# Splitting the opening batch of a DFT-and-GEGLU kernel by residue parity, with reordered loads and a later second batch

## The chip, the cores and the metric

The kernel runs on one core of one Trainium2 chip. The metric is the device time of one execution in microseconds; lower is better. All times in this text are microseconds unless another unit is named. Engines are called PE (matrix multiply), DVE (vector), ACT (activation), POOL (general purpose) and SP (which here only issues transfers).

## What is computed

The input x has 8 batches of 3008 rows with 256 channels. Each batch goes through a Fourier transform along the rows and one along the channels; the real part is then the input of a gated feed-forward block with 256 inputs, 1536 hidden units and 256 outputs.

```python
batch, seq, dim = (8, 3008, 256)
X = np.fft.fft(x, axis=1)
X = np.fft.fft(X, axis=2)
x = X.real.astype(np.float32).reshape(24064, 256)
g = x @ w_gate
gelu = 0.5 * g * (1.0 + erf(g * inv_sqrt2))
val = x @ w_val
out = (gelu * val @ w_out).astype(np.float32)
```

## The kernel before

**Row transform.** 3008 is 64 x 47. A batch is loaded in thirds (`load_x`, line 199) into three `xin` tiles. `fold_x` (211) adds and subtracts mirrored channels, which gives an even and an odd part of 128 channels each, and copies the two single channels (0 and 128). The first stage is `a_step(b, k)` (462): twelve steps for a batch, each with two matmuls against the table `G` and one copy into `S1`. The result has 128 rows for each of 24 slots. It goes through a scratch tensor `z` in HBM to change its layout: `z_write` (481) writes some of the 24 slots, `z_read` (489) reads thirds of it into `Ap`, every fourth partition from 0, 1 or 2. In `Ap` a group g of 0 to 31 is the row number modulo 32. The second stage is `b_steps(b, eo, q)` (499): a matmul of 47 columns against `TP`, `TQ`, `T0P` or `T0Q` for each group, eight groups into one PSUM bank (q is 0 to 3), for the even (`eo` 0) and odd part. The copies out of PSUM (`evac`, or `evac_top` and `evac_rest`) write `Y`, whose column is 32 m + g. All four q of a parity are needed for any 512 neighbouring columns of `Y`. For batch 0 the odd part is followed by one-column matmuls for the single channel; for later batches that row comes from `n_turn`, `n_step` and `n_read`.

**Channel transform.** It is folded into the weights: `gen_w` (397) multiplies the cast weights `wb` (`cast_w`, 391) by the table `CW` and gives `WE` and `WOP`, and `WOM`, which is `WOP` times minus two, so that it can be added onto a finished sum to turn the plus rows into the mirrored minus rows.

**Feed-forward.** Work is cut into units (b, chunk, fc): batch, chunk of `Y` columns, block of 128 hidden units; twelve units a chunk, three chunks a batch. `CH` (73) has the order of the chunks: the 481 columns from 1024, then 0 to 511, then 512 to 1023. A unit has five matmuls (`val_even`, `gate_minus`, `gate_plus`, `val_odd`), and six in the first chunk of batch 0, where the row `NQs` that DVE uses in the other units (`ev`, line 606) is not there yet. The products go to `h`; `plus` on DVE, `minus` on POOL. A chunk's second layer, `l2_steps` (689), starts after its twelfth unit, at six to eight matmuls against `Wo_sb` a unit.

**Order.** Every engine call goes through `_InOrder`, so each engine works in program order; a late operand stops everything behind it on that engine. SP's queue is in order too, and a transfer may wait in it for another transfer's landing. The loop over units (849) has the plan written out by hand: `extra` and `a_first` (828, 834) say at which unit of batch 0 a `gen_w` or an `a_step` of batch 1 is done; `first` and `evens` (840 to 846) say where the steps of `b_steps` are put (`fills`); `loads` (856) where the x of the batch after next is loaded.

**Opening.** Before the loop (766 to 827) the core loads x and a third of the weights, makes its tables, does the whole first and second stage of batch 0, and `gen_w` of the first 512 hidden units. `warm` issues matmuls whose result nobody uses; eight of them take the tile `gate`, read back from `z`, as weights. `cols_t` (247) works out column vectors from the partition number by rounding on DVE; `phase_t` and `sin_t` make the tables of the second stage from them. The transfers in this part are, in SP's order:

```python
z_read(0, 0); z_read(0, 1)        # gate read here
z_read(0, 2)
load_w(512, 1); load_w(512, 0); load_x(1, 0)
load_w(1024, 1); load_w(1024, 0); load_x(1, 1); load_x(1, 2)
```

`load_wo` (287) is issued on POOL after `cast_w(512)`, ahead of the folds of batch 1, which POOL does at units 0 to 11.

Of the kernel before, what the change touches and what calls it, by code (L numbers as in the profile page):

```python
# [9 lines left out]
FP32 = mybir.dt.float32  # L10
# [27 lines left out]
def kernel(  # L38
# [34 lines left out]
    CH = [(1024, NCOL - 1024), (0, 512), (512, 512)]  # L73
    MID = 24
# [26 lines left out]
    lone = const_pool.tile([128, NFC], BF16)  # L101

# [12 lines left out]
    col_q = const_pool.tile([128, 3], FP32)  # L115
    row_w = const_pool.tile([128, 3], FP32)
    row_b = const_pool.tile([128, 3], FP32)
    col_t = const_pool.tile([128, 1], FP32)
    col_k = const_pool.tile([128, 1], FP32)
    col_w = const_pool.tile([128, 1], FP32)  # L120
    col_m = const_pool.tile([128, 1], FP32)
    col_top = const_pool.tile([128, 1], FP32)
    col_bot = const_pool.tile([128, 1], FP32)
# [71 lines left out]
    def z_tile():  # L195
        return dram.tile([HJ, 128, C], BF16, tag="z", bufs=2, name="z")
# [14 lines left out]
    def fold_x(b, i, eng, a0=0, an=8, other=None):  # L211
# [8 lines left out]
        (other or eng).tensor_copy(  # L220
            _sub(xf, [[C, an], [128, 2]], o0), _sub(xt, [[C, an], [128, 2]], a0 * C))
# [17 lines left out]
    iota(col_q, [[0, 3]], 0, 1)  # L239
    for i in range(3):  # L240
        d = 4 << i
        pool.memset(row_w[:, i : i + 1], 1.0 / d)
        pool.memset(row_b[:, i : i + 1], (1.0 - d) / (2 * d))
    pool.tensor_tensor(col_q, col_q, row_w, op=ALU.mult)
    pool.tensor_tensor(col_q, col_q, row_b, op=ALU.add)

    def cols_t():
        f4, f8, f16 = (col_q[:, i : i + 1] for i in range(3))
        vec.tensor_scalar(col_q, col_q, MAGIC, None, op0=ALU.add)
        vec.tensor_scalar(col_q, col_q, MAGIC, None, op0=ALU.subtract)  # L250
        vec.scalar_tensor_tensor(col_t, f4, -4.0, col_p, op0=ALU.mult, op1=ALU.add)
        vec.scalar_tensor_tensor(col_bot, f8, -2.0, f4, op0=ALU.mult, op1=ALU.add)
        vec.scalar_tensor_tensor(f8, f16, -2.0, f8, op0=ALU.mult, op1=ALU.add)
        vec.scalar_tensor_tensor(col_j, col_t, 8.0, f16, op0=ALU.mult, op1=ALU.add)
        vec.scalar_tensor_tensor(col_j, f8, 24.0, col_j, op0=ALU.mult, op1=ALU.add)
        vec.tensor_scalar(col_j, col_j, 1.0 / N2, None, op0=ALU.mult)
        for o, b0 in ((0, 0.25), (2 * N2, 0.0)):
            vec.tensor_scalar(
                _sub(quat, [[1, 2 * N2]], o), _sub(col_bot, [[0, 2 * N2]], 0),
                0.25, b0, op0=ALU.mult, op1=ALU.add)  # L260
        vec.tensor_scalar(col_k, col_t, 3.0, None, op0=ALU.is_lt)
        vec.tensor_scalar(col_w, col_k, -TWO_PI, None, op0=ALU.mult)
        vec.tensor_tensor(col_bot, col_bot, col_k, op=ALU.mult)
        vec.tensor_tensor(col_top, col_k, col_bot, op=ALU.subtract)

    TO = 4 * N2
    iota(_sub(rowt, [[2 * N2, 2], [1, 2 * N2]], 0), [[0, 2], [1, 2 * N2]], 0, 0)
    iota(_sub(rowt, [[NJ, 2], [1, MID]], TO), [[0, 2], [1, MID]], 0, 0)
    iota(_sub(rowt, [[NJ, 2], [1, MID - 1]], TO + MID), [[0, 2], [1, MID - 1]], 1, 0)
    pool.memset(_sub(rowt, [[NJ, 2]], TO + NJ - 1), 0.0)  # L270
    pool.memset(_sub(quat, [[1, NJ]], TO), 0.25)
    pool.memset(_sub(quat, [[1, NJ]], TO + NJ), 0.0)
    TG = TO + 2 * NJ
    iota(_sub(rowt, [[NG, 2], [1, NG]], TG), [[0, 2], [-11, NG]], 0, 0)
    pool.memset(_sub(quat, [[1, NG]], TG), 0.25)
    pool.memset(_sub(quat, [[1, NG]], TG + NG), 0.5)
    wst = []

# [703 lines left out]
```

## Time and profile before

| what | value |
|---|---|
| median of 3 runs | 631.41 (631.33 to 631.5) |
| profiled execution | 629.75 |
| its span | 627.6 |
| first matmul of unit 0 | 28.60 |
| PE busy in the span | 606.0 |
| PE busy from 0 to 28.60 | 16.08 |
| PE busy from 28.60 to 54.20 | 24.02 of 25.60 |
| data moved from HBM and to it | 45.08 MB and 37.25 MB |

In the lines below, a row of the timeline has the start, the duration, the engine, the operation with what it writes and reads (out<-in), the shape, and after x how many of them were merged. In brackets stands the time that the engine was idle before, and what ended it. SPq and POOLq rows are issues of transfers, not the transfers themselves. Matmuls overlap, so the distance from one start to the next is the price of a matmul, not its duration. The profiled execution is one execution; the median belongs to others, and differs from it by 1.66.

### The profile page before, as it was taken

Reading aid. Unit: us, or ns where it says so; the run is one execution under the profiler, and the core shown is the slowest. Engines: PE = TensorE matmul, PEld = TensorE weight load, DVE = VectorE, ACT = ScalarE, POOL = GpSimd, SP = SyncE. Lnnn points to the kernel's source line nnn. Section 1 sums busy time; section 2 is a strip of 40 time slices with the busy share of each in tenths; the row PEclk is TensorE's granted clock in tenths of the full one; section 3 lists DMA queues with packets and bytes.
Section 4 is the critical chain, followed back from the end, with each engine's and each line's share of the span. In section 5 each row is a group of like instructions: output and inputs, shape, how many; then the busy total and the mean of one; then the engine's idle time right before and its main releaser. Section 6 shows DMA issues by size and latency. Waiting matters only on the chain.

```text
span 627.6 us, 12916 instructions
## 1 busy us (share of the span) xinstructions
PE 606.0 (97%) x4522; PEld 402.0 (64%) x4580; DVE 541.5 (86%) x654; ACT 471.8 (75%) x956; POOL 449.7 (72%) x480
## 2 busy tenths in 40 slices
PE   3899999999999999999999999999999999999997
PEld 2445666766666666766667666666667666666665
DVE  7688988898888998888988898889898898999991
ACT  8687778877788777877778777887778777766662
POOL 8296987769868789687787788687885555556552
PEclk9999999999999999999999999999999999999999
DMA  8997523653237512574246533366223612222113
GB/s 311 348 283 234 153 64 113 173 185 98 76 101 218 194 49 74 177 223 121 51 119 173 190 103 74 104 208 204 56 60 93 194 45 50 60 50 52 39 47 85
DMA packets 65458, 82.39 MB, mean 131 GB/s; under 512 B 8298, under 2 KB 58986, under 8 KB 62578
## 3 DMA queue, kind: packets, MB, share of 16 engines
q1 hardware_dynamic: 63682, 80.65, 42.4%
q0 software_dynamic: 1552, 0.79, 0.9%
q8 instruction: 36, 0.59, 0.4%
q14 instruction: 28, 0.23, 0.1%
q10 hardware_dynamic: 160, 0.13, 0.1%
HBM read 45.08 MB, written 37.25 MB: 131 GB/s over the span
## 4 chain that ended last, share of the span: by engine, by line
PE 91%; DMA 3%; DVE 3%; ACT 1%; issue 1%; POOL 0%; SPq 0%; ACTq 0%; DVEq 0%; POOLq 0%
PE ps_o L25 38%; PE ps_g L25 28%; PE ps_v L25 19%; PE ps_d L25 6%; DMA xin<-in_x_dram 3%; DVE h L25 1%; DVE S L25 0%; DMA z<-S 0%; ACT glp L25 0%; DVE xf L25 0%; ACT glm L25 0%; ACT S L25 0%; POOL xf L25 0%; SPq L25 0%; DVE WOM L25 0%
## 5 line engine op out<-in xcount | busy, mean ns | idle before, releaser
L25 POOL TENSOR_TENSOR h<-glm,dv 128x1024 bf16<-128x1024 bf16 (+1 forms) x138 | 290.9, 2108 | 153.2 <-DVE dv L25 110.0
L25 PE MATMUL ps_o<-Wo_sb,h 128*128 128x256 bf16 x2136 | 277.7, 272 | 0.5 <-DVE S L25 0.3
L25 DVE SCALAR_TENSOR_TENSOR ev<-nq,WN,ps_v 128x512 f32<-128x512 bf16 (+1 forms) x276 | 202.6, 734 | 62.3 <-PE ps_v L25 43.5
L25 ACT ACTIVATE glm<-ps_g 128x512 bf16<-128x512 f32 (+1 forms) x288 | 169.4, 588 | 110.0 <-PE ps_g L25 70.8
L25 PEld LDWEIGHTS <-h 128*128 128x128 bf16 x2208 | 210.8, 97 | 54.6 <-issue 0.9
L25 ACT ACTIVATE glp<-ps_g 128x512 bf16<-128x512 f32 (+1 forms) x288 | 169.9, 590 | 9.9 <-PE ps_g L25 0.3
L25 DVE TENSOR_TENSOR h<-glp,ps_v 128x1024 bf16<-128x1024 bf16 (+2 forms) x150 | 172.9, 1153 | 4.9 <-ACT glp L25 2.7
L25 DVE SCALAR_TENSOR_TENSOR dv<-ev,ps_v 128x1024 f32<-128x1024 f32 (+1 forms) x138 | 164.8, 1194 | 0.0
L25 POOL TENSOR_TENSOR xf<-xin 128x254 bf16<-128x254 f32 x168 | 118.3, 726 | 1.8 <-DMA xin<-in_x_dram 1.8
L25 PE MATMUL ps_g<-Y,WOM 128*128 128x512 bf16 (+1 forms) x288 | 107.7, 374 | 0.3
L25 PE MATMUL ps_v<-Y,WOP 128*128 128x512 bf16 (+1 forms) x288 | 107.7, 374 | 0.0
L25 PE MATMUL ps_v<-Y,WE 128*128 128x512 bf16 (+1 forms) x282 | 105.7, 375 | 0.1
L25 PE MATMUL ps_g<-Y,WOP 128*128 128x512 bf16 (+1 forms) x278 | 103.9, 374 | 1.7
L25 PE MATMUL ps_g<-Y,WE 128*128 128x512 bf16 (+1 forms) x249 | 92.9, 373 | 0.0
L25 PEld LDWEIGHTS <-WOP 128*128 128x128 bf16 x576 | 55.7, 97 | 52.8 <-ACT WOP L25 0.4
L25 PEld LDWEIGHTS <-WE 128*128 128x128 bf16 x576 | 56.0, 97 | 30.9 <-issue 0.6
L25 ACT ACTIVATE osb<-ps_o 128x512 f32<-128x512 f32 x93 | 54.8, 589 | 17.6 <-PE ps_o L25 13.6
L25 PEld LDWEIGHTS <-Ap 128*128 128x128 bf16 (+1 forms) x561 | 40.9, 95 | 33.8 <-issue 0.2
L25 ACT ACTIVATE S<-ps_d 128x512 bf16<-128x512 f32 x80 | 47.4, 593 | 0.1
L25 PEld LDWEIGHTS <-G 128*128 128x128 bf16 x213 | 20.8, 100 | 33.2 <-issue 11.8
L25 ACT ACTIVATE Y<-ps_d 128x192 bf16<-128x192 f32 (+4 forms) x142 | 34.0, 340 | 0.5 <-PE ps_d L25 0.5
L25 PEld LDWEIGHTS <-WOM 128*128 128x128 bf16 x300 | 29.2, 97 | 4.9
(140 smaller groups left out, 262.7 us busy)
## 6 DMA issues: line engine op xcount, KB each, us to landing
out_dram<-osb SPq DMA_DIRECT2D x358, 64.0 KB
xin<-in_x_dram SPq DMA_DIRECT2D x16, 1024.0 KB
Ap<-z SPq DMA_DIRECT2D x24, 512.0 KB
xin<-in_x_dram SPq DMA_DIRECT2D x8, 896.0 KB
z<-S SPq DMA_DIRECT2D x7, 768.0 KB
z<-S SPq DMA_DIRECT2D x8, 512.0 KB
nq<-nrow SPq DMA_DIRECT2D x8, 376.2 KB
z<-S SPq DMA_DIRECT2D x11, 256.0 KB
```

What stands on the lines that cost most here:

```text
L25: return lambda *a, **k: self._tc.keep_in_program_order(call(*a, **k))
```

## The change

The change concerns batch 0, the opening, and where batch 1's stages are put; a few of its parts hold for all batches.

- The scratch `z` is split in two by the parity of the row (`z_tile(half)`); a half is written from every second partition of `S1`. `Ap` holds the sixteen even groups first, then the odd ones. For all batches each `z_write` and `z_read` becomes one transfer for each half. In the opening only half 0 is written and read at first; half 1 is written in one transfer later, and read back in three.
- Batch 0 has its own chunk order and its own column order (`CH0`, `evac_first`, `halved_windows`, `store_apart`): columns 0 to 511 of `Y` are the even groups, 512 to 1023 the odd ones, and the rest is as it was. So the first chunk needs q 0 and 1 only. `b_steps` for q 2 and 3 is done at units 7 to 10. The stores of these chunks go to every second row of the output.
- Group 0, whose two column ranges now go to different places, is done by a matmul in each of two banks (q 0 and q 1).
- The column vectors of `cols_t` come from five matmuls of one row (`prow`, made on POOL by `rows_t`); most of the DVE operations of `cols_t` and the tile `gate` are gone.
- On POOL `cols_c` and `phase_c` move ahead of the folds, the tables and the clearing of `Ap` behind the first of them; `cast_w(1024)` comes directly after `cast_w(512)`, and `load_wo` moves to unit 4.
- In the opening `WOM` is made from `WOP` in SBUF after all four `gen_w`, and one copy moves from ACT to DVE. There are fewer `warm` matmuls: 7 after the first stage instead of 5, 2 and 10 within it, and 3 and 4 instead of 4 and 8 before the second stage.
- The weights of the hidden units 512 to 1535 are loaded ahead of x of batch 1; half 1 of `z` is written after the first third of that x.
- Batch 1's `a_step`s are at units 9 to 18 instead of 4 to 13, its `z_read`s at units 15, 17 and 20, its first `b_steps` at unit 22 instead of 21, and `n_first(0)` at unit 8 instead of 0. `load_x(2, ...)` is at units 8, 15 and 20 instead of 8, 12 and 18.
- The last rows of batch 0's first two chunks are gathered in a tile `aside` on POOL.

```diff
     CH = [(1024, NCOL - 1024), (0, 512), (512, 512)]
+    CH0 = [(0, 512), (1024, NCOL - 1024), (512, 512)]
...
-    def z_tile():
-        return dram.tile([HJ, 128, C], BF16, tag="z", bufs=2, name="z")
+    def z_tile(half):
+        return dram.tile([HJ, 64, C], BF16, tag=f"z{half}", bufs=2, name=f"z{half}")
...
+    def rows_t():
+        row = lambda i, pat, off=0: _sub(prow, pat, 128 * i + off, 0, 1)
+        iota(row(0, [[16, 8], [8, 2], [4, 2], [1, 4]]), [[1, 8], [24, 2], [0, 2], [8, 4]], 0, 0)
+        slots = [[8, 16], [4, 2], [1, 4]]
+        for i, (base, sign) in enumerate(((0, 1), (0, 1), (1, -1))):
+            iota(row(1 + i, slots), [[0, 16], [sign, 2], [0, 4]], base, 0)
+        pool.memset(row(4, [[1, 129]]), 1.0)
+        pool.memset(row(2, [[128, 3], [4, 32]], 3), 0.0)
 
     def cols_t():
...
+        ps = ps_o()
+        for i in range(5):
+            pe.matmul(ps[:, i : i + 1], _sub(prow, [[1, 128]], 128 * i, 0, 1),
+                      _sub(prow, [[1, 1]], 640, 0, 1), start=True, stop=True)
+        vec.tensor_copy(cols, ps[:, :5])
+        vec.tensor_scalar(col_j, cols[:, 0:1], 1.0 / N2, None, op0=ALU.mult)
+        vec.tensor_scalar(col_w, cols[:, 4:5], -TWO_PI, None, op0=ALU.mult)
+
...
+        copy = act.copy if eng is None else eng.tensor_copy
+        on_half(ps, copy((WE, WOP)[eo][:, i, fs], ps))
+        if eo:
+            if f0:
+                on_half(ps, vec.tensor_scalar(
+                    WOM[:, i, fs], ps, col_m, None, op0=ALU.mult))
+            else:
+                odd_evacs.append(lambda: vec.tensor_scalar(
+                    WOM[:, i, fs], WOP[:, i, fs], col_m, None, op0=ALU.mult))
 
...
+            st[b]["z"] = [z_tile(half) for half in range(2)]
+        S1 = st[b]["S1"]
+        for half in halves:
+            z = st[b]["z"][half]
+            dst = ap_replace(
+                z[0:1, 0, :], ap=[[C, 64], [64 * C, nj], [1, C]], offset=z[j0, 0:1, :].offset)
+            rows = _sub(S1, [[C, nj], [1, C]], j0 * C, half, 64)
+            p_step, p_count = rows.ap[0]
+            src = ap_replace(
+                rows, ap=[[2 * p_step, p_count]] + [list(a) for a in rows.ap[1:]],
+                offset=rows.offset)
+            sync.dma_start(out=dst, in_=src)
+
+    def z_read(b, third, halves=(0, 1)):
+        n = NG // 2 * C
+        for half in halves:
+            z = st[b]["z"][half]
+            src = ap_replace(
+                z[0:1, 0, :], ap=[[n, 32], [1, n]], offset=z[8 * third, 0:1, :].offset)
+            p_step = Ap[:, :, :].ap[0][0]
+            dst = ap_replace(
+                Ap[:, :, :], ap=[[4 * p_step, 32], [1, n]],
+                offset=Ap[:, :, :].offset + third * p_step + half * n)
+            sync.dma_start(out=dst, in_=src)
...
+                pos = (8 * q + gi) % 16 + NG // 2 * (q // 2) if gi < 8 else 0
+                g = 2 * (pos % 16) + pos // 16
+                w = _sub(Ap, [[1, 1 if m1 else 128]], pos * C + eo * 128)
...
+                    lo, hi = (MID, N2) if gi else (0, MID)
                     keep((pe.matmul(
-                        ps[r, 0:N2], w, t[:, 0:N2], start=True, stop=True)))
-                    keep(pe.matmul(ps[r, 8 * N2 : 8 * N2 + 1], w, t[:, N2 : N2 + 1],
-                                         start=True, stop=True))
+                        ps[r, o + lo : o + hi], w, t[:, lo:hi], start=True, stop=True)))
+                    if gi == 0:
+                        keep(pe.matmul(ps[r, 8 * N2 : 8 * N2 + 1], w, t[:, N2 : N2 + 1],
+                                             start=True, stop=True))
...
+        gh, first, n = q // 2, q % 2 * 8, 9 if q == 1 else 8
+
+        def part(lo, hi, halved):
             ps = box["ps"]
             if Ys[b] is None:
                 Ys[b] = Y_tile()
-            copy(
-                _sub(Ys[b], [[32, MID], [1, 8]], eo * YW + 8 * q),
-                _sub(ps, [[1, MID], [N2, 8]], 0))
+            f = 1 if q == 0 and lo >= MID else 0
+            p = first - (1 if q == 1 and lo >= MID else 0)
+            nn = (n if lo >= MID else 8) - f
+            at = 512 * gh + 16 * lo + p if halved else \
+                32 * lo + 2 * p + (1 - gh if lo >= MID else gh)
+            m, s = (16, 1) if halved else (32, 2)
+            copy(_sub(Ys[b], [[m, hi - lo], [s, nn]], eo * YW + at),
+                 _sub(ps, [[1, hi - lo], [N2, nn]], lo + f * N2))
+
+        def evac_first():
+            if gh:
+                part(0, 32, True)
+            else:
+                part(0, MID, True)
+                part(MID, 32, True)
 
         def evac_rest():
...
+            part(32, N2, False)
             if q == 0:
-                copy(
-                    _sub(Y, [[32, n2]], eo * YW + 32 * MID + 31), ps[:, MID:N2])
-                copy(
-                    _sub(Y, [[1, 1]], eo * YW + NCOL - 1), ps[:, 8 * N2 : 8 * N2 + 1])
-
-        steps = [mm(gi, False) for gi in range(8)]
+                copy(_sub(Ys[b], [[1, 1]], eo * YW + NCOL - 1),
+                     box["ps"][:, 8 * N2 : 8 * N2 + 1])
+
+        order = [*range(1, n), 0] if q == 0 else range(n)
+        steps = [mm(gi, False) for gi in order]
...
+    def halved_windows(ci):
+        h = hs[(0, ci)]
+        gh = CH0[ci][0] // 512
+        row = lambda m: 64 * m + (1 if gh else 2 * (m >= MID))
+        out = [(h, 128 * w, (row(8 * w), 8), None) for w in range(4)]
+        out += [(h, 128 * w, (T - row(8 * (8 - w) - 1) - 30, 8), None) for w in range(4, 8)]
+        if gh == 0:
+            pool.tensor_copy(aside[:, :, :], h[:, :, 896:1024])
+            return out[:7]
+        return out
...
     for i in (1, 0):
         load_w(0, i)
+    cols_c()
+    for t in range(NCH):
+        phase_c(t)
+    def clear(i):
+        pool.memset(Ap[:, 16 * i : 16 * i + 16, :].bitcast(FP32), 0.0)
+
...
     phase_g(0)
     phase_g(1)
-    cols_c()
     sin_g(0)
     sin_g(1)
     turn_g()
-    pool.tensor_copy(col_k, _sub(reds[1], [[1, 1]], 0))
     for i in range(3):
-        fold_x(0, i, vec, other=pool)
-        if i < 2:
-            pool.memset(Ap[:, 16 * i : 16 * i + 16, :].bitcast(FP32), 0.0)
-        else:
-            for t in range(NCH):
-                phase_c(t)
+        fold_x(0, i, vec, single=False)
+        if i == 0:
+            singles(0)
+            singles(1)
+            rows_t()
+            clear(0)
+            singles(2)
+            tables()
+            clear(1)
+        elif i == 2:
+            cols_t()
         for k in range(4 * i, 4 * i + 4):
             a_step(0, k)
-            if i == 0 and k == 3:
-                z_write(0, 0, 8)
-            elif i and k % 2:
-                z_write(0, 2 * k - 2, 4)
-        warm((5, 2, 10)[i])
-    z_read(0, 0)
-    z_read(0, 1)
-    gate = work.tile([128, 128], BF16, tag="gate", bufs=1, name="gate")
-    sync.dma_start(out=gate[:, :], in_=ap_replace(
-        st[0]["z"][0:1, 0, :], ap=[[C, 128], [1, 128]], offset=st[0]["z"][0:1, 0, :].offset))
-    z_read(0, 2)
+            if k % 2:
+                z_write(0, 2 * k - 2, 4, (0,))
+    warm(7)
+    z_read(0, 0, (0,))
+    z_read(0, 1, (0,))
+    z_read(0, 2, (0,))
     for i in (1, 0):
         load_w(512, i)
-    load_x(1, 0)
     for i in (1, 0):
         load_w(1024, i)
+    load_x(1, 0)
+    z_write(0, 0, HJ, (1,))
+    for i in range(3):
+        z_read(0, i, (1,))
     load_x(1, 1)
     load_x(1, 2)
     reduce_c()
-    cols_t()
-    pt = phase_t()
+    quats()
     sin_c()
     cast_w(0)
+    pt = phase_t()
     gen_w(0, 1, 0, ps_g)
     gen_w(0, 1, 1, ps_vh)
+    gen_w(0, 0, 0, ps_g, vec)
     sin_t(*pt)
-    gen_w(0, 0, 0, ps_g)
     gen_w(0, 0, 1, ps_vh)
     act.activation(col_f[:, :], col_p[:, :], AF.Gelu)
-    warm(4)
-    warm(8, gate[:, :])
+    for w in odd_evacs:
+        w()
+    odd_evacs.clear()
+    warm(3)
+    warm(4, TP)
     later_evacs = []
     for eo in range(2):
-        for q in range(4):
-            steps, evac, evac_top, evac_rest = b_steps(0, eo, q)
+        for q in range(2):
+            steps, evac, evac_first, evac_rest = b_steps(0, eo, q)
             for s in steps:
                 s()
-            if eo:
-                evac_rest()
-                later_evacs.append(evac_top)
-            else:
-                evac()
+            evac_first()
+            later_evacs.append(evac_rest)
     cast_w(512)
-    load_wo()
-    extra = {1: [lambda: cast_w(1024)], 13: [gen_tf]}
-    for n, turn in ((0, (ps_o, ps_d, ps_o, ps_d)), (1, (ps_o, ps_o, ps_d, ps_o))):
+    cast_w(1024)
+    extra = {4: [load_wo], 13: [gen_tf]}
+    for n, turn in ((0, (ps_o, ps_d, ps_o, ps_d)), (1, (ps_o, ps_d, ps_o, ps_d))):
         for j, bank in enumerate(turn):
-            extra.setdefault(4 * n + j, []).append(
+            extra.setdefault(4 + j if n else (1, 2, 2, 3)[j], []).append(
                 lambda f0=512 + 512 * n, i=1 - j // 2, eo=j % 2, bank=bank: gen_w(f0, i, eo, bank))
-    extra[7].append(gen_wn)
-    a_first = {4: (0,), 5: (1,), 12: (10,), 13: (11,), 14: (12,), 15: (13,)} | {
-        8 + j: (2 + 2 * j, 3 + 2 * j) for j in range(4)}
+    extra.setdefault(10, []).append(gen_wn)
+    a_first = {9: (0,), 10: (1, 2), 11: (3, 4)} | {12 + j: (5 + j,) for j in range(7)}
+    reads_first = {15: 0, 17: 1, 20: 2}
 
     NU = len(units)
     PER = NU // B
...
-    first = {23: ["n"], 21: [(1, 0, 0, 4)], 22: [(1, 0, 4, 8)]} | {
+    first = {22: [(1, 0, 0, 4)], 23: [(1, 0, 4, 8)]} | {
         23 + q: [(1, q, 0, 8)] for q in range(1, 4)}
+    first[24].append("n")
     plan = [first | evens, later | evens]
+    second_half = {7: (1, 2), 8: (1, 3), 9: (0, 2), 10: (0, 3)}
...
-            loads = (0, 14, 19) if b else (8, 12, 18)
+            loads = (0, 14, 19) if b else (8, 15, 20)
...
-                    if k in (8, 10, 13):
+                    if b and k in (8, 10, 13):
                         z_read(b + 1, (8, 10, 13).index(k))
+                if b == 0 and i in reads_first:
+                    z_read(1, reads_first[i])
```

## The prediction

> **What bounds the kernel now.** I read the page first, then the busy time by stretches, then the timeline of the opening and of the SP queue, and the trace's gaps on PE. One profiled execution took 629.75 us, its span 627.6; the median of the runs is 631.41, so 1.66 is added to whatever the sum gives for that execution.
>
> ```profile
> span 627.6 us, 12916 instructions
> PE 606.0 (97%) x4522; PEld 402.0 (64%) x4580; DVE 541.5 (86%) x654; ACT 471.8 (75%) x956; POOL 449.7 (72%) x480
> ```
> ```profile
> 0.00:28.60 28.60, 16.08 (x159) 9.26 (x161) 22.13 (x65) 20.53 (x47) 16.66 (x45) 1.00 0.91 324
> 28.60:54.20 25.60, 24.02 (x146) 11.99 (x147) 21.40 (x38) 21.24 (x42) 23.80 (x48) 1.00 0.84 256
> 75.00:150.00 75.00, 74.57 (x574) 50.54 (x581) 65.37 (x73) 58.25 (x121) 60.08 (x65) 1.00 0.44 130
> ```
> Columns: stretch, its length, busy PE, PEld, DVE, ACT, POOL (instructions), granted clock, DMA share, GB/s. From 75 on PE is busy 74.57 of 75: the end moves only by what PE does or waits for. 12.5 of the idle time lies before 28.60, where the DMA share is 0.91; another 1.58 until 54.20.
>
> ```profile
> 8.88 0.58 PE L25 MATMUL ps_g<-xf,G 128*128 128x256 bf16 x2 [8.88 <-DVE xf L25]
> ...
> 12.46 0.38 PE L25 MATMUL ps_g<-xf,G 128*128 128x256 bf16 x2
> ...
> 14.95 2.02 POOL L25 CAST wb<-wst 128x1024 bf16<-128x1024 f32 x2
> ...
> 15.96 0.68 DVE L25 CAST S<-ps_o 128x512 bf16<-128x512 f32 x1
> ...
> 23.60 1.90 PE L25 MATMUL ps_d<-G,gate 128*128 128x512 bf16 x8 [2.30 <-DMA gate<-z]
> ...
> 25.17 3.38 PEld L25 LDWEIGHTS <-Ap 128*128 128x128 bf16 x99 [0.16 <-issue]
> ...
> 28.60 0.38 PE L25 MATMUL ps_v<-Y,WE 128*128 128x481 bf16 x1
> ...
> 29.17 0.36 PE L25 MATMUL ps_g<-Y,WOP 128*128 128x481 bf16 x1
> ```
> The first stage's last result is copied by 16.64, but its use as Ap starts at 25.17: write to z and read back. Then 99 steps take 3.43, and unit 0 starts.
>
> ```profile
> 17.21 1.17 SPq L25 DMA_DIRECT2D Ap<-z  x2
> 18.43 0.57 SPq L25 DMA_DIRECT2D gate<-z  x1
> 19.88 0.45 SPq L25 DMA_DIRECT2D Ap<-z  x1
> ...
> 29.52 0.31 SPq L25 DMA_DIRECT2D nrow<-Y  x1
> 37.59 0.36 SPq L25 DMA_DIRECT2D nq<-nrow  x1
> ...
> 56.56 0.37 SPq L25 DMA_DIRECT2D z<-S  x1
> ...
> 63.50 0.48 SPq L25 DMA_DIRECT2D Ap<-z  x1
> ```
> The SP queue shows how long a small transfer takes behind large ones: nq could be issued only 8.07 after nrow, and batch 1's last Ap read 6.94 after its z write.
>
> **Opening.** The six folds on DVE end at 13.67 as before (row 6.38 7.29). The third group of a_steps then needs four pairs at 0.22 (pitch at 12.46, 12.68, 12.90) or 0.43 (pitch at 8.88 to 10.11), since warm-ups go, and copies of 0.6: last S1 at 15.3 to 16.1; I take 16.0. The last write of half 0 has 4 x 64 x 512 B; the last whole write took 3.11 from issue to landing behind others, so 1.5 to 3.1, taken 2.4. The last half read replaces one that took at most 5.3 (19.88 to 25.17) behind two double ones and gate: 2.3 to 5.3, taken 3.1. Ap's first half is there at about 21.6 (limits 19.1 to 24.5). There are 54 steps instead of 99 (18 even, 36 odd), at 3.43/99 = 0.035: 1.9, until 23.5.
>
> The other way into unit 0 is POOL and ACT. POOL now does phase_c (2.43) and col_c before the folds, but rows_t (four iotas, two memsets, 1.0 from rows of 0.1 to 0.3), two clears of 1.82, singles and tables after x lands, so cast_w(0) (2.02) ends at about 18.3 against 16.97. Four gen_w at 0.43 follow (20.0), two ACT copies of 0.6, sin_t (1.1, from 21.69 to 22.83), one copy, the table load (1.28): 23.2, then four odd Y copies at 0.26 (row of 1.03 for four): WOP of unit 0 at 24.5 against 29.17. The two ways end within a microsecond of each other, so an earlier Ap alone gains nothing more. On DVE cols_t loses nine small operations (18.22 to 20.16 without quat, 1.6) to five one-row matmuls which wait only for POOL; WOM from WOP in SBUF takes 0.43 (the f32 row of that width) instead of 0.74. Unit 1 starts at about 24.9 against 30.01: **-5.1** (limits -3.5 to -6.1).
>
> [...]
>
> **Work brought into the stream.** A second-half step costs 0.026 there (start to start at 70.45 to 70.53): 16 even and 32 odd ones, 48 x 0.026 = +1.25. The gen_w of unit 0 comes later: +0.43. The first chunk is 512 wide with six matmuls a unit, the second 481 with five: 0.216 - 0.203 is 0.013 (pitches at 54.17 and 46.17), 12 x (6 - 5) x 0.013 = +0.15. Group 0 is split over two banks, one matmul more per parity and batch: 14 x 0.026 = +0.36. Together **+2.2**.
>
> **Costed at nothing.** ACT copies per batch fall by two (0.28 each): ACT idles a quarter. The aside copy (128x1536; hx of 512 took 0.61, so 1.8) fits into POOL's 5.27 idle before 60.01; without it the folds of batch 2 come 1.8 later. z transfers doubled in number add six issues of 0.4 to 0.5 per batch on SP, whose queue is not on the path; if it were, stores would be 2.6 late, which only delays osb.
>
> **Waits.** (a) Half 1. SP issues w512, w1024, x(1,0), then z half 1 and its reads, then x(1,1), x(1,2) and, since POOL alone holds it, x(2,0), and only then nrow and nq. A megabyte takes about 2.7 (390 GB/s in these slices). From 21.0 (0.6 ahead of Ap's landing): three megabytes to 29.1, half 1 written by 32.6, read by 37.0. Unit 7, its first user, stands at 35.6 without waits: 0.9 on average, 0 to 3. (b) x(1,0) comes to POOL at 29.9, its folds (1.49 a pair) end at 35.9, and only then load_wo is issued. It took 15.2 to land before, much of it beside x; here 12 to 15 gives 48 to 51. nrow is queued behind x(2,0), which ends near 44.4; nq, issued on its landing, took up to 6.7 before (37.59 to 44.3, where the DMA slices fall silent), 4 to 6.7 here: 49 to 51. PE would reach the first layer-2 step at 46.6 without waits, 47.6 with two thirds of the 1.58 that this stretch idles now. ev of unit 12 waits for nq, and behind it on DVE stand h of unit 11 and an S copy; behind layer 2 on PE stands everything. I take 49.0, unit 13 at 49.9 against 54.17, which contains (a). (c) Batch 1's last a_step is at unit 18, its Ap first used at unit 22: 7.9 us. Copy 1.0, writes 4.3 (3.11 for the 256 KB row, 1.2 for 256 KB more at 210 GB/s), x(2,2) between (0.9 MB, 2.3), reads 2.1 (half of a batch's third at that pace, and landing): 9.7, and less where they overlap. 0 to 1.9, taken 0.9; behind it on PE all else, and on POOL n_turn and minus.
>
> **Sum** at unit 13: 54.17 - 49.9 = 4.3 early. Five a_steps of 0.22 are still to do: -1.1. The narrower chunk gives back 11 x 5 x 0.013 = 0.7. Split group: -0.36. Wait (c): -0.9. Left 2.6. From the parts: 5.1 - 2.2 = 2.9, with new waits almost offset by the idle time they replace. 629.75 - 2.6 = 627.15 for the profiled run, **628.8** as a median.
>
> **Rivals.**
> 1. *The transfers set the pace* (0.19): Wo and nq land at 50 to 51, so unit 13 starts at 51.0, and (c) costs 1.4: 3.2 - 1.1 + 0.7 - 0.36 - 1.4 = 1.0: 630.4. For it: SP's new order, and 8.07 from nrow to nq. Against: DMA stands nearly idle at 45 to 50 now, so there is room.
> 2. *Slower* (0.18): nq, put behind x(2,0), and Wo share the engines as at 37 to 41, where slices show 200 to 230 GB/s against 390. Then x(2,0), Wo and nq end about 3 later than in the sum, at 53.5; unit 13 starts at 54.4, after the old kernel's, and with (c) at 1.9: -0.2 - 1.1 + 0.7 - 0.36 - 1.9 = -2.9: 634.3. It decides from unit 13 at 51.5 (where 2.66 of lead are just spent). Against: nq was not waited for at all before, its first use at 53.16 being 8.9 behind the silence at 44.3.
> 3. *A slow array* (0.08): all a_steps, gen_w and the 54 steps at half pace: 0.9 + 1.7 + 1.9 more, of which about half lies under POOL and ACT: unit 1 at 27.1. PE reaches layer 2 at 49.8 instead of 49.0: 629.6.
> 4. *The opening does not shorten*, since ACT's chain (copies, sin_t, table load, Y) starts from POOL's late cast (0.05): unit 1 at 28.5, PE at layer 2 at 51.2: 631.0. For it: cast_w(0) comes 1.3 later. Against: ACT was idle 1.43 before TP, which cols_t's matmuls shorten.
>
> **How the numbers follow.** The forecast itself (0.50) has 626.5 to 629.9. A measurement of this kernel tells 0.2%, 1.26 us, from no change. Faster: most of the forecast (0.48), all of rival 3 but a little (0.06), a third of rival 1 (0.06), and a little of 4: 0.62. Same: rest of 1 and parts of the others: 0.18. Slower: rival 2 and tails of (c): 0.20. The range leaves out gains beyond 5 us and the worse half of rival 2: 626.2 to 633.2.
>
> **What would show it.** Right: the first matmul of a unit near 23.5 to 24.5; 54 Ap steps in one run ahead of it; the odd-half steps in units 7 to 10 with a PE gap before the first of 0 to 2; unit 13 near 50; a PE gap of about 1 near unit 22 ended by Ap<-z; from 80 on the same rows as before, about 2.6 earlier. Wrong: WOP of unit 0 after 27; PE waiting for Wo_sb or DVE ev for nq more than 3; gaps in later batches at Ap, which would mean that halved transfers cost something in every batch and not once.

## Result and profile after

The changed kernel takes 646.5 us (median of 4 runs, 645.36 to 649.13) against 631.4 for the kernel before beside it: 1.0253 times as long, 95% interval 1.0213 to 1.0292. The forecast was 628.8. The profiled run of the changed kernel is the longest of the four, 649.13, with a span of 647.0, 19.4 more than the span before; its mean granted clock is 0.986. (The other three have 0.983, 0.991 and 0.991 and took 647.4, 645.59 and 645.36.)

The first lines are from the head of the profile's page of the changed kernel; the table is its busy time by stretches, with the columns of the one shown for the kernel before.

```profile
span 647.0 us, 12951 instructions
...
PE 612.6 (95%) x4531; PEld 403.8 (62%) x4587; DVE 542.2 (84%) x645; ACT 476.9 (74%) x944; POOL 452.6 (70%) x476
```
```profile
0.00:28.60 28.60, 16.20 (x116) 8.60 (x118) 22.51 (x54) 21.38 (x51) 19.29 (x42) 1.00 0.78 281
28.60:54.20 25.60, 19.95 (x118) 8.77 (x118) 15.76 (x27) 15.27 (x29) 17.86 (x34) 0.87 0.89 255
54.20:75.00 20.80, 17.10 (x126) 10.66 (x127) 15.02 (x21) 12.24 (x24) 8.29 (x12) 0.92 0.37 111
75.00:150.00 75.00, 69.28 (x509) 45.69 (x512) 57.57 (x66) 53.61 (x109) 58.74 (x69) 0.95 0.44 135
```

PE had 1.58 idle from 28.60 to 54.20 before; now it is 5.65, then 3.70 up to 75 and 5.72 up to 150. The granted clock, 1.00 in all four stretches before, is 0.87, 0.92 and 0.95. The starts of the units say where the lead was won and lost:

| start of unit | before | after | after - before | lost since the row above |
|---|---|---|---|---|
| 1 | 30.01 | 26.68 | -3.33 | |
| 9 | 45.56 | 47.52 | +1.96 | 5.3 |
| 13 | 54.17 | 62.97 | +8.80 | 6.8 |
| 22 | 71.45 | 82.07 | +10.62 | 1.8 |
| 25 | 77.64 | 96.92 | +19.28 | 8.7 |
| end of span | 627.6 | 647.0 | +19.4 | 0.1 |

Behind unit 25 nothing more is lost. The opening is early, and all of the loss lies between units 1 and 25. These are PE's rows there with the seven largest waits, from the timeline (start, length, operation, in brackets the idle time before it and what ended it):

```profile
40.84 0.21 PE L25 MATMUL ps_o<-TQ,Ap 128*128 128x47 bf16 x2 [1.99 <-DMA Ap<-z]
...
44.98 0.24 PE L25 MATMUL ps_d<-TQ,Ap 128*128 128x47 bf16 x2 [0.76 <-DVE WOM L25]
...
52.73 0.21 PE L25 MATMUL ps_d<-TP,Ap 128*128 128x47 bf16 x2 [2.21 <-DVE S L25]
...
54.85 0.74 PE L25 MATMUL ps_d<-CW,wb 128*128 128x1 bf16 x24 [0.89 <-ACT Y L25]
...
61.87 0.39 PE L25 MATMUL ps_d<-xf,G 128*128 128x256 bf16 x2 [0.83 <-DVE S L25]
...
87.40 0.24 PE L25 MATMUL ps_d<-TQ,Ap 128*128 128x47 bf16 x2 [4.18 <-DMA Ap<-z]
...
95.70 0.40 PE L25 MATMUL ps_d<-NA,TF 128*48 128x31 f32 x6 [1.26 <-ACT Y L25]
```

In their order: half 1 of Ap late (unit 7), a bank still held by WOM's copy (8), a bank held by the copy of the second batch's k=0 (10), `gen_wn` behind the copies of Y (10), an a_step behind the copy of an earlier one (12), the second batch's Ap late (22), and the n step behind the copies of Y (24). The chain that ended last goes through the two waits for Ap:

```profile
23.00 11.81 DMA z<-S
35.98 4.72 DMA Ap<-z
...
77.53 4.92 DMA z<-S
82.46 4.80 DMA Ap<-z
```

Half 1 was 11.81 on its way to z, behind w512, w1024 and x(1,0), and 4.72 on its way back. The second batch's last third needed 9.7 for both.

Why the opening gained 3.33 instead of 5.1 is on POOL (timeline), with the two DVE rows that ran beside its last cast, and then on PE:

```profile
10.17 2.04 POOL L25 IOTA prow<- 1x128 bf16 x4
12.17 0.56 POOL L25 MEMSET prow<- 1x129 bf16 x2
12.54 1.88 POOL L25 MEMSET Ap<- 128x2048 f32 x1
14.38 0.24 POOL L25 CAST xf<-xin 128x16 bf16<-128x16 f32 x1
...
17.33 2.26 POOL L25 CAST wb<-wst 128x1024 bf16<-128x1024 f32 x2
```
```profile
17.55 1.13 DVE L25 SCALAR_TENSOR_TENSOR red<-red 128x256 f32<-128x256 f32 x1
18.61 1.12 DVE L25 TENSOR_SCALAR red<-red 128x256 f32<-128x256 f32 x1
19.77 0.43 DVE L25 SCALAR_TENSOR_TENSOR red<-red 128x256 f32<-128x256 f32 x1
```
```profile
14.68 0.58 PE L25 MATMUL ps_g<-xf,G 128*128 128x256 bf16 x2 [1.17 <-POOL xf L25]
...
20.70 0.39 PE L25 MATMUL ps_g<-wb,CW 128*128 128x512 bf16 x1 [1.12 <-ACT CW L25]
```

rows_t takes 2.6 where 1.0 was priced, and the clear stands behind it too, so the third singles come at 14.38 and the third a_steps wait 1.17. Then the same operation on `red` takes 1.13 beside POOL's cast and 0.43 when the cast is over; CW comes late and PE waits again.

### The profile page after: what moved, and what is told of

It reads as the page before. It is cut to its first block, busy times and chain, and to the rows that moved or that the text cites. A ratio compares the mean times of both kernels' runs of the same rounds, so it can differ in the third digit from the quotient of the medians.

```text
span 647.0 us, 12951 instructions
## 1 busy us (share of the span) xinstructions
PE 612.6 (95%) x4531; PEld 403.8 (62%) x4587; DVE 542.2 (84%) x645; ACT 476.9 (74%) x944; POOL 452.6 (70%) x476
## 4 chain that ended last, share of the span: by engine, by line
PE 88%; DMA 6%; DVE 2%; ACT 1%; issue 1%; SPq 1%; POOL 1%; DVEq 0%; ACTq 0%; POOLq 0%
PE ps_o L25 37%; PE ps_g L25 27%; PE ps_v L25 18%; PE ps_d L25 6%; DMA z<-S 3%; DMA Ap<-z 1%; DMA xin<-in_x_dram 1%; SPq L25 1%; DVE h L25 1%; DVE S L25 0%; ACT glp L25 0%; POOL prow L25 0%; DVE dv L25 0%; ACT glm L25 0%; POOL Ap L25 0%
## 5 line engine op out<-in xcount | busy, mean ns | idle before, releaser
L25 PE MATMUL ps_v<-Y,WE 128*128 128x512 bf16 (+1 forms) x283 | 107.2, 379 | 0.1
L25 PEld LDWEIGHTS <-Ap 128*128 128x128 bf16 (+1 forms) x578 | 44.6, 97 | 49.8 <-issue 9.6
L25 ACT ACTIVATE S<-ps_d 128x512 bf16<-128x512 f32 x77 | 45.6, 592 | 0.9 <-PE ps_d L25 0.9
L25 ACT ACTIVATE Y<-ps_d 128x192 bf16<-128x192 f32 (+4 forms) x133 | 41.5, 409 | 0.4 <-PE ps_d L25 0.3
L25 PE MATMUL ps_d<-xf,G 128*128 128x256 bf16 x164 | 31.5, 274 | 2.1 <-DVE S L25 2.1
```

Of the source, the lines that this page charges most:

```text
L25: return lambda *a, **k: self._tc.keep_in_program_order(call(*a, **k))
```

## Experiments

Each kernel ran beside the kernel before (median 629.85 in the runs of e1 to e4, 631.25 in e5 to e8, 630.17 for e9, 631.52 for e10, 631.4 for e11 to e13). Ratios are to it. Diffs are against the changed kernel unless another is named.

**Is it the slow array?** e1 fills the waits at units 7 and 22 with matmuls that nobody uses.

```diff
+                    if i == 7:
+                        fills.append(lambda: warm(10))
...
+                    if b == 0 and i == 22:
+                        fills.append(lambda: warm(20))
```

> The changed kernel with 10 dummy matmuls of 512 columns ahead of the first second-half step in unit 7, and 20 ahead of batch 1's first step in unit 22, both inside waits for Ap (1.99 and 4.2 us there). Nothing else moves, and Ap lands when it did. Theory A, the clock: the records of the changed kernel show the array at 0.5 from 42.16 to 48.99 and from 86.53 to 93.36, behind these two waits, each worth up to 3.4 us; then the dummies keep it at 1.0 there and the time falls by 4 to 7 us (to about 640). Theory B, the waits alone: the half clock is hidden by other waits, and the time stays within 1 us of 646.5.

Measured 645.69, 1.0253 (1.022 to 1.0286). In the profiled execution the half clock behind units 7 and 22 is gone (clock 0.994), and units 22 to 25 take 12.2 instead of 14.85; behind unit 10's wait there is still a period of half clock, 6.83 long instead of 3.41. The median falls by 0.8 only and the ratio not at all. The slow array is real here (clock 0.50 from 42.16, 55.81 and 86.53 in the changed kernel, behind waits of 1.99, 2.21 and 4.18), but the 4 to 7 expected from the first and the last of these periods are not there; a gain of 2 or less cannot be told from four runs.

**Is it half 1's way through z?** e2 writes half 1 ahead of w1024 and reads it ahead of x(1,0).

```diff
+    z_write(0, 0, HJ, (1,))
     for i in (1, 0):
         load_w(1024, i)
-    load_x(1, 0)
-    z_write(0, 0, HJ, (1,))
     for i in range(3):
         z_read(0, i, (1,))
+    load_x(1, 0)
```

> The changed kernel with half 1 of z written ahead of the weights of units 1024 and its reads ahead of x of batch 1. Theory A (half 1 is late because of its place in SP's queue, where 11.8 us pass between its issue at 23.00 and its landing): Ap's half 1 lands about 5 us earlier, PE waits for nothing in unit 7, the clock stays at 1.0 there, and 4 to 7 us go; the later weights may cost up to 2 at unit 4. Theory B (units 8 to 12 lose their time on the one bank ps_d, whoever comes late): the wait at unit 7 goes, but the waits on DVE S and ACT Y at units 8 to 11 stay, and 2 to 3 us go.

Measured 646.8, 1.0263 (1.0235 to 1.029). The wait at unit 7 is gone, the one behind it at unit 8 grew to 1.66, and the one at unit 22 stays (4.36). One wait went and the median stayed. In the profiled execution the units 1 to 9 do take less, 18.0 instead of 20.8, but unit 1 starts at 29.24 instead of 26.68: the array ran at half clock there from 19.55, in the opening, for 6.83 (mean granted clock of that execution 0.983). So what half 1's wait is worth by itself stays open.

**Is it the bank?** In e3 the copy of k=0 goes to ACT. On DVE it stood behind two h and the copies of Y, and unit 10's b_steps need its bank.

```diff
-        if b == 0 and k % 2 == 0 and k >= 8 or b == 1 and k in (0, 3, 5, 7, 9):
+        if b == 0 and k % 2 == 0 and k >= 8 or b == 1 and k in (3, 5, 7, 9):
```

> The changed kernel with the copy of batch 1's first a_step on ACT instead of DVE. In the changed kernel PE stood 2.21 us in unit 10 for that copy, which is queued on DVE behind two h products and two Y copies, since the next b_steps take the same bank ps_d. Theory B (the bank): the wait falls from 2.2 to about 0.7, and the clock window from 55.81 to 59.23 may stay at 1.0: 1.5 to 3.5 us less. Theory A (late transfers alone set the pace): no more than 0.5 us, because nq and Wo land at 54 to 56 anyway.

Measured 642.52, 1.0195 (1.0165 to 1.0226): 4.0 less than the changed kernel by the medians, 3.7 by the ratios (whose intervals just overlap), for one copy. The 2.21 before unit 10's steps is 0.26 in the row of the same steps:

```profile
48.34 0.21 PE L25 MATMUL ps_d<-TP,Ap 128*128 128x47 bf16 x2 [0.26 <-ACT S L25]
```

This bank wait is shown. The half clock behind it (from 55.81) is gone too in the profiled execution, and so is the one behind unit 7 (from 42.16), so the 3.7 are not the wait alone.

**Is it x(2) in the queue at unit 22?** e4 moves the loads of x(2,1) and x(2,2).

```diff
-            loads = (0, 14, 19) if b else (8, 15, 20)
+            loads = (0, 14, 19) if b else (8, 18, 22)
```

> The changed kernel with the second and third part of x of batch 2 loaded at units 18 and 22 instead of 15 and 20, behind the reads of batch 1's Ap. Theory A (the wait of 4.2 us at unit 22 is due to these loads ahead of z and Ap in the queue): Ap lands 3 to 4 us earlier, the wait falls below 1, the clock stays at 1.0 from 86 on, and the time falls by 6 to 9 us. Rival (the write and the read of the last third need that long by themselves, 9.7 us from copy to landing in 7.9): the wait falls by 1 to 2 us only, the half clock stays, and the time falls by 1 to 2.

Measured 648.06, 1.0294 (1.0261 to 1.0328), and unit 22 waits 4.37. It was not a clean test: x(2,1) at unit 18 was issued at 74.85, right ahead of the write. e7 repeats it properly.

**What does the later second batch cost by itself?** e5 is the kernel before, with whole z transfers and its own opening, and only the second batch's places (with their banks, reads, folds and n step) from the change.

```diff
-    a_first = {4: (0,), 5: (1,), 12: (10,), 13: (11,), 14: (12,), 15: (13,)} | {
-        8 + j: (2 + 2 * j, 3 + 2 * j) for j in range(4)}
+    a_first = {9: (0,), 10: (1, 2), 11: (3, 4)} | {12 + j: (5 + j,) for j in range(7)}
+    reads_first = {15: 0, 17: 1, 20: 2}
```

> The kernel before, whole z transfers and old opening, with only the second batch's work in the places that the change gives it. If the placement is what costs (theory): PE waits 3 to 4.5 us for Ap at unit 22 as in the changed kernel (4.18), about 2 for single a_steps on DVE's copies, 1.3 for the n step, so 636 to 639. If the halved transfers are what makes the way through z long (rival): the wait at unit 22 is at most 1 and the time 631 to 633.

Measured 639.12, 1.0126 (1.0108 to 1.0144): 7.9 come with the placement alone (the x(2) loads and the folds moved with it), against 15 for the whole change. The timeline of PE in e5 has the wait at unit 22 though nothing is halved:

```profile
80.14 0.20 PE L25 MATMUL ps_d<-T0Q,Ap 128*128 128x47 bf16 x2 [3.38 <-DMA Ap<-z]
...
88.31 0.40 PE L25 MATMUL ps_d<-NA,TF 128*48 128x31 f32 x6 [1.05 <-ACT Y L25]
```

**Do the late weights matter?** e6 is the kernel before with w1024 loaded ahead of x(1,0).

```diff
-    load_x(1, 0)
     for i in (1, 0):
         load_w(1024, i)
+    load_x(1, 0)
```

> The kernel before with one thing changed: the last third of the weights is loaded ahead of the next x's first part. If the order of these loads matters by itself, x(1,0) and with it Wo come some 2.5 us later and PE waits for Wo at layer 2: 633 or more. If it is hidden (theory, since layer 2 had Wo early before): 631 to 632.

Measured 630.82, 0.9999 (0.9983 to 1.0015): no difference.

**Four waits away at once.** e7 has e2 and e3, the third singles ahead of the clear, and x(2,1), x(2,2) in units 21 and 24; e8 adds earlier a_steps, the last in unit 16, with banks and copies to match.

```diff
-            clear(0)
             singles(2)
+            clear(0)
...
-            loads = (0, 14, 19) if b else (8, 15, 20)
+            loads = (0, 14, 19) if b else (8, 21, 24)
```

> The changed kernel with four waits taken away at once: k=0's copy on ACT (2.21 at unit 10 gone), half 1 through z ahead of the last weights and x (1.99 at unit 7 gone), the third singles ahead of the clear (third a_steps 1.0 earlier, unit 1 at 25.5 to 26.2 instead of 26.68), both later parts of x(2) behind the third read. If the queue behind x(2,1) made unit 22 wait, that wait falls from 4.2 to 0 to 2; if it is the way through z itself, it stays over 3. Sum of the gains 2.2 + 1.8 + 0.8 + 2 to 3: 638 to 641 by the theory of separate waits; 643 or more if a removed wait only comes back later.

```diff
-    a_first = {9: (0,), 10: (1, 2), 11: (3, 4)} | {12 + j: (5 + j,) for j in range(7)}
-    reads_first = {15: 0, 17: 1, 20: 2}
+    a_first = {4: (0,), 5: (1,), 9: (2,), 10: (3, 4), 11: (5, 6), 12: (7,), 13: (8,), 14: (9,),
+               15: (10,), 16: (11,)}
+    reads_first = {13: 0, 15: 1, 18: 2}
```

> The kernel e7 with the second batch's a_steps earlier: two in units 4 and 5, the last in unit 16 instead of 18, and its reads in units 13, 15 and 18. By the theory that two units (4 us) are what unit 22 lacks: no wait there, 635 to 639. By the rival, that banks o and d are full in units 4 to 10 and an earlier step only moves the wait: new gaps of 1 to 3 us in units 4 to 10 and no gain on e7.

e7: 646.47, 1.0231 (1.0203 to 1.0259). e8: 643.47, 1.0187 (1.0165 to 1.0209). In e7 unit 1 starts at 26.3, and unit 22 still waits 3.87 with no x near the write: the theory that x(2) was in the way falls, the way through z itself is too long for the place. In e8 that wait is gone, so two units were what was missing; but k=0 in unit 4 waits 5.21 for its folds, since x(1,0) now comes late. What ate e7's gain is in none of the theories. PE and DVE in e7 (timelines):

```profile
58.22 0.58 PE L25 MATMUL ps_v<-Y,WOM 128*128 128x512 bf16 x1 [4.54 <-DVE h L25]
```
```profile
49.80 0.17 DVE L25 CAST WNb<-ps_d 128x12 bf16<-128x12 f32 x1
50.00 7.58 DVE L25 CAST WN<-WNb 128x12 f32<-128x12 bf16 x1
57.50 0.67 DVE L25 TENSOR_TENSOR h<-glp,ps_v 128x512 bf16<-128x512 bf16 x1
```

A copy of 12 numbers a row took 7.58, and h stood behind it. (WN holds the sums of the gate weights that DVE needs, with nq, for `ev`.) The copy had taken 0.53 in the kernel before and 1.13 in the changed one; in e10 it takes 9.83.

**Rebuilding the order.** e9 and e10 keep the halves and set the order around them anew: other places for cast_w(0), the clears, rows_t, w512, Wo, and a_steps in units 5 to 15.

```diff
-    a_first = {9: (0,), 10: (1, 2), 11: (3, 4)} | {12 + j: (5 + j,) for j in range(7)}
-    reads_first = {15: 0, 17: 1, 20: 2}
+    a_first = {5: (0,), 7: (1,), 9: (2,), 10: (3, 4), 11: (5, 6), 12: (7, 8), 13: (9,), 14: (10,),
+               15: (11,)}
+    reads_first = {12: 0, 14: 1, 17: 2}
```

> The changed kernel's opening and halves with the order around them rebuilt: cast_w(0) ahead of the clears on POOL, w512 loaded between the half-0 writes, half 1 written ahead of x(1,0) and the last weights, Wo issued right behind cast_w(512), a_steps of the second batch in units 5 to 15 (last write three units earlier than in the changed kernel), its b_steps and n step where the kernel before has them. If what the change lost lies in the order alone (theory): unit 1 at 24.3 to 25.5 (30.0 before), no wait over 1 us for Ap at units 7 or 21, unit 13 at 50 to 53, 625 to 630. If half 1's steps, the split group and banks o and d in units 5 to 11 cost more than the opening gains however they are ordered (rival): unit 13 at 54 or later and 631 to 636.

```diff
+            clear(0)
             singles(0)
             singles(1)
-            rows_t()
-            clear(0)
+            clear(1)
             singles(2)
+            cast_w(0)
+            rows_t()
             tables()
-            clear(1)
```

> As e9, with what its trace showed mended: both clears ahead of the casts (Ap's reads waited for the second clear until 20.2), rows_t and cols_t behind the third a_steps, the last weights again ahead of x(1,0) so that their cast comes early, Wo issued in unit 2, one a_step per unit from 5 to 9, the sums for the gate weights in unit 6. By the theory (order alone): unit 1 at 24.0 to 25.5, unit 5 at most 9 later than unit 0, unit 13 at 50 to 53, 625 to 630. By the rival (the halves' own work in units 7 to 10 and a full DVE and ACT there cost what the opening gains): unit 1 as said but unit 13 at 54 or later, 631 to 635.

Both missed: 639.95, 1.0146 (1.0116 to 1.0176), and 641.66, 1.0165 (1.014 to 1.0189). In e9 Ap's reads were issued only at 20.2, when the second clear ended. In e10, w512 between the z writes delayed the third read to 21.6, from 18.3 in e7. Unit 1 started at 29.4 and 28.6; in both profiled executions 3.41 of half clock fall into the opening (from 25.70 and 24.86; mean granted clocks 0.991 and 0.989). Later e9 waits 2.85 for `wb` (40.12). And e10's DVE, POOL and PE show the copy of WN at its worst:

```profile
43.34 9.83 DVE L25 CAST WN<-WNb 128x12 f32<-128x12 bf16 x1
53.08 0.68 DVE L25 TENSOR_TENSOR h<-glp,ps_v 128x512 bf16<-128x512 bf16 x1
```
```profile
51.74 1.39 POOL L25 TENSOR_TENSOR xf<-xin 128x254 bf16<-128x254 f32 x2
53.09 0.19 POOL L25 CAST xf<-xin 128x4 bf16<-128x4 f32 x1
```
```profile
53.81 0.59 PE L25 MATMUL ps_v<-Y,WOM 128*128 128x512 bf16 x1 [6.91 <-DVE h L25]
```

The second fence is POOL's last fold in e10. The copy ended at 53.17, beside the last cast of POOL's row of folds (53.09 to 53.28).

**The copy of WN alone.** e11 is e7 with one line changed.

```diff
-        vec.tensor_copy(WN[:, :], WNb[:, :])
+        act.copy(WN[:, :], WNb[:, :])
```

> e7 with one line changed: the copy of WN from WNb (12 numbers a row) goes to ACT. On DVE it took 0.53 us in the kernel before, 1.13 in the changed one, 7.58 in e7 and 9.83 in e10, and in e10 it ended within 0.1 us of POOL's last fold. Theory (this copy can't run beside POOL's folds, and everything on DVE stands behind it): the wait of 4.54 at unit 12 of e7 goes, 640 to 642.5 instead of 646.5. Rival (unit 12 waits for nq or Wo, issued at 50.7 and 45.1): the wait stays over 3 and the time at 645 to 648.

Measured 642.68, 1.0198 (1.0161 to 1.0235), 3.8 less than e7 by the medians, with intervals that overlap; the wait of 4.54 is gone. nq and Wo, issued at 50.3 and 43.8 against 50.7 and 45.1 in e7, are cleared.

**The rebuilt order, mended.** e12 is e10 with that line, w512 behind the half-0 reads again, x(1,0) ahead of half 1, and a_steps in units 6 to 16, besides smaller moves (the cast of w1024, Wo, `gen_wn`, banks); e13 moves the last two S copies of the second batch in e12 from DVE to ACT (the second diff is against e12).

```diff
+    a_first = {6: (0,), 7: (1,), 8: (2,), 9: (3,), 10: (4,), 11: (5, 6), 12: (7,), 13: (8,),
+               14: (9,), 15: (10,), 16: (11,)}
+    reads_first = {13: 0, 14: 1, 18: 2}
```

> The rebuilt order of e10 with that copy on ACT, w512 behind the half-0 reads again (between the z writes it delayed the third read from 18.3 to 21.6), x(1,0) ahead of half 1, and a_steps in units 6 to 16. Theory (with waits and the long copy gone only the work itself is left): unit 1 at 24.5 to 26, unit 13 at 50 to 53, no PE wait over 1 us up to unit 25, 625 to 631. Rival (units 7 to 12 stay over 2.2 us each, since DVE and ACT are full there): unit 13 at 54 to 57, 631 to 636.

```diff
-        if b == 0 and k % 2 == 0 and k >= 8 or b == 1 and k in (3, 6):
+        if b == 0 and k % 2 == 0 and k >= 8:
```

> e12 with the second batch's two S copies that DVE still did (k=3 in unit 9, k=6 in unit 11) on ACT. Theory (in the units where b_steps or a_steps share a bank, a copy behind h and Y on DVE holds PE, and nothing else is left): the waits of 2.21 before 49.69 and 0.82 before 56.96 go, and with the first the half clock behind it (50.21 for 3.41); 633.2 - 2.2 - 0.8 - up to 1.7 = 628.5 to 630.2, so level with the kernel before or up to 0.4% under it. Rival (the halves' steps and split copies fill ACT, so the wait only moves to ACT): a new wait of 1 to 2 at the same places and 632 to 634.

e12: 633.2, 1.0035 (1.0022 to 1.0048). e13: 629.74, 0.9981 (0.997 to 0.9992), median of 12 runs: 2.6% under the changed kernel and 0.2% under the one before. The 0.2% go with the clock: the runs of the kernel before with a mean granted clock of 0.998 or more took 629.55 to 630.62 beside e13, those with 0.997 or less 631.33 to 632.38. e13's runs (0.997 to 1.000) took 629.15 to 630.95, and both profiled spans are 627.6. At the same clock the two kernels are level. The one copy that e12 still had in front of a b_step on its bank, and e13's same place:

```profile
49.69 0.21 PE L25 MATMUL ps_d<-TP,Ap 128*128 128x47 bf16 x2 [2.21 <-DVE S L25]
```
```profile
47.29 0.21 PE L25 MATMUL ps_d<-TP,Ap 128*128 128x47 bf16 x2 [0.26 <-ACT S L25]
```

In e13 unit 1 starts at 25.06 (4.95 earlier than before) and unit 13 at 54.1 (54.17 before): the lead of the opening is spent in between. The stretch from unit 1 to unit 13 by busy time, e13 and then the kernel before:

```profile
25.10:54.10 29.00, 25.33 (x181) 12.47 (x183) 19.49 (x34) 22.87 (x46) 22.78 (x41) 1.00 0.90 260
```
```profile
30.00:54.20 24.20, 22.66 (x138) 11.40 (x140) 21.00 (x36) 20.02 (x39) 22.43 (x46) 1.00 0.83 250
```

PE works 2.7 longer there and idles 3.67 instead of 1.54.

## Why the prediction was wrong

**The opening** (-5.1, limits -3.5 to -6.1) was right in its mechanism and mis-sized: -3.33, just outside the limits. The term that failed is rows_t at 1.0 (2.6 measured, and it stood with a clear ahead of the third singles) together with operations on DVE priced without POOL's cast beside them (1.13 beside it, 0.43 behind it). e13, with POOL's order mended, has -4.95.

**Work brought into the stream** (+2.2) is about right: e13 has 2.7 more PE work in units 1 to 13. By the prediction's own prices this stretch should have 2.0 more (the steps 1.25, `gen_w` 0.43, the wider chunk 12 x 6 x 0.013 = 0.94, three a_steps fewer -0.66), so it is priced some 0.7 low.

**Costed at nothing** and **Waits** failed, and this is the step that turned the sign. The sum took the new waits as almost offset by the idle time they replace; in the changed kernel 3.33 of lead became 19.28 of lag between units 1 and 25. Three things:

1. *Wait (c)* was taken as 0.9 (0 to 1.9) and is 4.18. The window of 7.9 was too long: the last a_step is the last work of its unit (76.19 to 76.57), and PE asks for Ap at 83.22, 6.65 later. The way was 10.7 (until 87.26) instead of 9.7: 1.0 of copy and issue, 4.92 written, 4.80 read. It is there without the halves (e5) and without x(2) near the write (e7), so neither is needed for it, and two units more remove it (e8).
2. *The moved a_steps' banks and copies* were not priced at all. I counted their PE time as moved, and did not ask who uses banks o and d in units 9 to 18 and who copies them out. k=0's copy alone is worth about 3.7 (e3, the clock behind it included); single a_steps behind DVE's copies wait another 0.6 to 0.8 three times, and the n step 1.26 behind the copies of Y. With the wait (c), the placement alone makes 7.9 (e5). The rest of the 15 is not split further: the waits do not add up one by one, as e7 shows.
3. *Half 1* (a) waited 1.99, inside 0 to 3. But what stands behind it at unit 8 was left out: 0.76, and 1.66 in e2, where half 1 is there in time.

*Wo and nq* (b): nq was issued at 52.27 and Wo landed at 54.4, later than the 48 to 51 I gave, and no PE row waited for them, since PE came even later (unit 13 at 62.97). The slower rival named nq and Wo, so it had the side right and the place wrong; e11 clears them. That it gave 634.3 at worst shows the same gap: it too had no term for banks.

**The slow array** was the third rival at 0.08. No run shows by itself that fewer warm-ups bring it. The kernel before has both pitches in its opening (0.43 a pair from 8.88, 0.22 from 12.46), and there 2.30 idle before 23.60 had not brought the slow one: the next eight matmuls took 1.90. In the changed kernel the third a_steps still have 0.38 to 0.43 a pair (starts 14.68 to 15.91), and half clock appeared behind the waits at units 7, 10 and 22 (0.50 for 6.83, 3.41 and 6.83). It is part of the loss in the profiled execution: of the 8.7 lost in units 22 to 25 the two waits make 5.4, and e1 without the half clock takes 2.65 less there. But e1 takes two of the three periods away and its median gains 0.8, within the noise. How much of the 15 the slow array makes is not settled; e13, whose waits are all under 1 us from unit 0 on, has a clock of 1.000.

**From unit 25 on** the same time as before, as foreseen: 0.1 lost, and no cost of halved transfers in later batches.

**What the opening's lead is worth.** Even with the waits mended, e13 reaches unit 13 at 54.1, not at the 49.9 of the sum: of its 4.95, 2.7 go into added PE work and 2.1 into idle time that the kernel before did not have there.

## What to carry to other kernels

A step that is moved takes a bank, a copy on some engine's queue and a transfer with it: list who holds that bank and what stands ahead of that copy in the new place before the gain is counted, and measure a window from where the work ends in its unit, not from where the unit starts. When taking away a wait leaves the time unchanged, look for the next wait on the same chain, down to the smallest operation on a queue, and compare the granted clock of the two executions: here a copy of 12 numbers a row hid the gain of e7 and e10, and half clock in the opening what units 1 to 9 gained in the profiled execution of e2. An opening made 4.95 us shorter was worth 0.2% at the end, and nothing at the same clock, since the work taken out of it came back in a stream that had no room.

## What the runs showed of the hardware

**A copy of 12 numbers a row on DVE took up to 9.83 us beside POOL's folds.** WN from WNb, both in SBUF, took 0.17 to 1.56 on DVE in most kernels, 7.58 in e7 and 9.83 in e10, both times while POOL ran folds back to back; 0.20 on ACT in e11. Folds beside it do not always do this: POOL was folding in the kernel before too, where the copy took 0.53. In e10 it stood through some twenty POOL instructions; in e7 it ended at 57.58, with POOL's folds going on to 58.37. What held the copy was not tried by itself, and why it took so long only in e7 and e10 stays open; e11 shows only that the copy was to blame (with it on ACT the wait of 4.54 is gone).

**A gap of 2.3 us on PE had half clock behind it in one execution and full clock in another.** e5 has the opening of the kernel before, with 2.26 idle before 23.51. The stretches around it, in e5 and in the kernel before (2.30 idle before 23.60):

```profile
21.20:24.62 3.42, 1.16 (x7) 0.52 (x7) 2.49 (x7) 2.95 (x7) 0.00 (x0) 1.00 0.95 348
24.62:28.03 3.41, 3.41 (x55) 2.42 (x53) 1.26 (x6) 1.78 (x6) 1.02 (x1) 0.50 1.05 408
```
```profile
21.20:24.60 3.40, 1.10 (x6) 0.51 (x6) 2.54 (x7) 2.89 (x7) 0.00 (x0) 1.00 0.96 343
24.60:28.00 3.40, 3.40 (x88) 2.67 (x85) 1.67 (x9) 2.14 (x7) 1.30 (x2) 1.00 1.07 416
```

The same wait, once 0.50 and once 1.00 behind it, with PE busy for 1.16 and for 1.10 in the stretch ahead. In the changed kernel half-clock periods start at 42.16, 55.81 and 86.53 and last 6.83, 3.41 and 6.83; PE was busy for 1.42, 2.19 and 0.11 in the 3.41 ahead of them, and a fourth starts at 646.32, at the end of the span. The kernel before has one such period, at the end of its span, from 626.63. How little PE worked in the stretch ahead does not tell the cases apart: in the changed kernel it was busy for 1.49 from 48.99 to 52.40, and full clock followed. What decides it is not shown by these runs.

**What a half-clock period costs.** The 64 runs of the kernel before that stood beside e1 to e13 fall into two groups: 28 with a mean granted clock of 0.998 or more took 628.8 to 630.6 (median 629.8), 36 with 0.997 or less took 631.1 to 632.6 (median 631.6). The 1.75 between them is about half of 3.41. The traced execution of the kernel before is of the first group (0.999). In that of e6, at 0.996, the array has half clock from 23.63 for 3.41 (the eight matmuls on `gate` take 3.52 at 23.73, against 1.90 in the kernel before), and unit 1 starts at 31.75 instead of 30.01; that the second group has such a period in its opening fits, but no trace of it shows it.
